# A block-causal attention and feed-forward kernel: the whole program in a scheduling block ordered by a simulated timeline, with the attention steps recorded scores first and attn*v in three steps

## The chip, the cores and the metric

The kernel runs on one core of a Trainium2 chip. The metric is the device time of one execution in microseconds (us); lower is better. Five engines work in the core, each through its own list of instructions in a fixed order, and they meet through semaphores: PE (TensorE, matmuls and transposes), DVE (VectorE), ACT (ScalarE), POOL (GpSimd) and SP (SyncE, which here issues all DMAs). An instruction that waits holds up everything behind it on its engine.

## The reference

```python
B, H, S, D = 8, 8, 576, 64                       # q, k, v; blocks of 64 for the mask
scores = q @ k.T / sqrt(D)                       # per batch and head
scores = where(block_i >= block_j, scores, -1e9)
attn = softmax(scores)                           # row maximum, exp, divided by its sum + 1e-9
x = concat_heads(attn @ v)                       # 4608 tokens x 512
h = x @ w_in                                     # 512 x 2048
g = where(h >= 1, h, where(h <= -1, 0, (h + 1)**2 / 4))
out = g @ w_out                                  # 2048 x 512
```

## The kernel before, in words

**Arithmetic.** Matmuls in full precision are slow on PE, so most operands are split into a high part of a shorter format (float32r) and the rest, and two or three matmuls take the place of one. The weights are split this way in the kernel (`convert`, L156, on ACT, DVE and POOL, in 64 pieces), mostly while the first batches are in work.

**Attention.** The unit is a *pair*: two heads (j = 0, 1) of one batch, so there are 8 x 4 = 32 pairs. Per head the 576 query rows make four tiles of 128 (in the groups 0: tiles 0 and 1, 1: tile 2, 2: tile 3), and the last 64 rows of both heads make one group more ("last"). So a pair has seven groups. Each goes through a chain:

- `scores` (L494) or `scores_last` (L518): matmuls into a PSUM bank `ps_s` (L482, L485; 24 of them in a pair); row maxima `nm` on DVE (L505, L529); exp on ACT (L509, L535) into `pr`, of which there are three buffers; sum and reciprocal `sm` on DVE (L491, L492); scaling on DVE (L515, L541). Then the result is copied by DMA into `prr` (L250, `as_float32r`), called the hop here.
- `turn` (L556) or `turn_last` (L572): PE transposes `prr` into a bank `ps_t` (L552); ACT and DVE split it into the tiles `pa` and `pb` (L545, L547). The last group's final 64 columns (the corner) go through a bank of their own into `pcs`.
- `attn_v_first` (L631) and `attn_v(0)`, `attn_v(1)` (L640): PE multiplies by v into `ps_av` (L591); ACT and DVE add two halves into `x32` (L613, L614), and `store_x` (L647) writes the split result to `xh`, `xl`, the input of the second part.

q and k of a pair are transposed too (`ps_qk`: L401, and L442 in `turned_last`, L437, for the last 64 rows). Pairs of the batches 0 and 1 are *plain* (no splits, other steps); those of the batches 2 to 7 are *far*, and their q and k are first copied from DRAM to DRAM (`fetch`, L273). From the middle of the second batch on, all these banks come from one ring of three (`work_bank`, L80). A bank is free again when the DVE or ACT instructions that read it are done.

**Feed-forward (FFN).** Nine chunks of 512 tokens, 16 pieces (fc) of 128 hidden columns each: `ffn_in` (L763) does 12 matmuls of 512 columns into the one bank `ph` (L770); ACT and DVE make `t` from it (L779, L780, L783), ACT and POOL split that into `gh`, `gl` (L784, L785); `ffn_out` (L790) does 12 matmuls into four banks `po` (L794, L799). So a piece has 24 matmuls. Chunk c takes tokens of batch c and for c over 0 also of batch c - 1; it can be done only when batch c is through the attention, all four pairs of it (the matmuls of one pair's channels, three of the first piece, can go before).

**Order.** `attention_steps` (L663) records each pair in eight steps, with the tail of the pair before and the head of the one after mixed in. From step 36 on (four pairs and four steps), one FFN step, that is half a piece, is recorded behind each attention step (L838 to L852): four pieces a pair, 16 a batch. The framework's scheduler then turns the recorded program into one list per engine; it may move instructions where dependencies and buffers allow. In the kernel before, this is done with its default method for the whole program.

Of the kernel before, what the change touches and what calls it, by code (L numbers as in the profile page):

```python
# [8 lines left out]
F32 = mybir.dt.float32  # L9
# [14 lines left out]
def block_attn_then_ffn(  # L24
# [61 lines left out]


    ident_f = ffn.tile([P, 512], F32, tag="t", name="ident_f")[:, :P]
    make_identity(nc, ident_f)
    ident_r = const.tile([P, P], F32R, tag="ident", name="ident_r")  # L90
    nc.vector.tensor_copy(ident_r, ident_f)
    ident = ident_r.bitcast(F32)

    xh = const.tile([P, NCC, RING], F32R, tag="xh", name="xh")
    xl = const.tile([P, NCC, RING], F32R, tag="xl", name="xl")
    wih = const.tile([P, NCC, DF], F32R, tag="wih", name="wih")
    wil = const.tile([P, NCC, DF], F32R, tag="wil", name="wil")

    copies = [dram.tile([B, H, S, D], F32, tag=f"raw{x}", name=f"raw{x}") for x in "qk"]
    wo_split = dram.tile([NFC, P, 2, DM], F32, tag="wo_split", name="wo_split")  # L100
# [3 lines left out]
    qa = const.tile([P, 2, QW], F32R, tag="qa", name="qa")  # L104
    qb = const.tile([P, 2, QW], F32R, tag="qb", name="qb")
    ka = const.tile([P, 2, S], F32R, tag="ka", name="ka")
    kb = const.tile([P, 2, S], F32R, tag="kb", name="kb")

    def last_blocks(t_):

        view = t_[:, :, SM : SM + BLK]
        if t_.shape[2] == S:
            return view
        part, (_, two), cols = view.ap
        return bass.AP(tensor=view.tensor, offset=view.offset, ap=[part, [QW + BLK, two], cols])


    mrow = att1.tile([NTL, 2, S], F32R, tag="pb0", name="mrow")


    pcs = [const.tile([P, 2, BLK], F32R, tag=f"pcs{i}", name=f"pcs{i}") for i in range(2)]
    vsr = [const.tile([P, NTL + 1, 2, D], F32R, tag=f"vsr{j}", name=f"vsr{j}") for j in range(2)]

    mtmp = ffn.tile([P, 512], F32, tag="t", name="mtmp")
    msel = ffn.tile([P, 512], F32, tag="t", name="msel")
    nc.vector.memset(mtmp, 0.0)
    nc.vector.memset(msel[:NTL], 0.0)
    nc.gpsimd.affine_select(
        out=msel[:NTL, : NTL * BLK].rearrange("p (t c) -> p t c", c=BLK),
        in_=msel[:NTL, : NTL * BLK].rearrange("p (t c) -> p t c", c=BLK),  # L130
        compare_op=ALU.not_equal, fill=1.0, base=0,
        pattern=[[-1, NTL], [0, BLK]], channel_multiplier=1,
    )
    sel = msel[:NTL, : NTL * BLK].rearrange("p (t c) -> p t c", c=BLK)
    for side in range(2):
        nc.vector.tensor_copy(mrow[:, side, :512], mtmp[:NTL, :512])
        nc.vector.tensor_copy(mrow[:, side, 512:S], mtmp[:NTL, : S - 512])
    rows = mrow[:, :, :SM].rearrange("p s (t c) -> p s t c", c=P)
    nc.vector.tensor_copy(rows[:, 0, :, :BLK], sel)
    nc.vector.tensor_scalar_mul(rows[:, 1, :, BLK:], sel, MASKED)  # L140
    for t_ in (qa, qb):
        nc.vector.tensor_copy(
            t_[:, :, SM:], mtmp[:, : 2 * (QW - SM)].rearrange("p (h c) -> p h c", h=2)
        )
    for t_ in pcs:
        nc.vector.tensor_copy(t_[BLK:], mtmp[BLK:, : 2 * BLK].rearrange("p (h c) -> p h c", h=2))
    for t_ in vsr:
        nc.vector.tensor_copy(
            t_[BLK:, NTL, :, :], mtmp[BLK:, : 2 * D].rearrange("p (h c) -> p h c", h=2)
        )  # L150
    for j in range(2):
        nc.sync.dma_start(qa[D:KA, j, :S].bitcast(F32), mrow[:, 0, :].bitcast(F32))
        nc.sync.dma_start(ka[D:KA, j, :].bitcast(F32), mrow[:, 1, :].bitcast(F32))


    def convert(n, source, hi, lo, done):  # L156

        if n < BORROW and n % 2:
            bits = ffn.tile([P, CW, 2], I32, tag="t", name="bits")
            work = ffn.tile([P, 2, CW], F32, tag="gl", name="work")  # L160
        else:
            bits = conv.tile([P, CW, 2], I32, tag="bits", name="bits")
            work = conv2.tile([P, 2, CW], F32, tag="work", name="work")
        nc.sync.dma_start(bits, source.bitcast(I32).rearrange("p (n t) -> p n t", t=2))
        top, mag = work[:, 0, :], work[:, 1, :].bitcast(U32)
        low = bits[:, :, 0]


        nc.scalar.mul(top, bits[:, :, 1].bitcast(F32), 2.0**-112)
        nc.scalar.mul(low, low.bitcast(U32), 2.0**-29)  # L170
        nc.vector.tensor_scalar(
            out=top, in0=top, scalar1=F32_TOP, scalar2=-F32_TOP, op0=ALU.min, op1=ALU.max
        )
        nc.vector.tensor_scalar(
            out=mag, in0=top.bitcast(U32), scalar1=3, scalar2=None, op0=ALU.logical_shift_left
        )
        nc.vector.scalar_tensor_tensor(
            out=mag, in0=top.bitcast(U32), scalar=0x80000000, in1=mag,
            op0=ALU.bitwise_and, op1=ALU.bitwise_or,
        )  # L180
        yield
        w32 = mag.bitcast(I32)
        nc.gpsimd.tensor_tensor(out=w32, in0=w32, in1=low, op=ALU.add)
        w32 = w32.bitcast(F32)
        nc.scalar.copy(hi(), w32)
        yield
        nc.gpsimd.tensor_tensor(out=lo(), in0=w32, in1=hi().bitcast(F32), op=ALU.subtract)
        if done:
            done()

    def weight_pieces():

        for f0 in range(0, DF, CW):
            fs = slice(f0, f0 + CW)
            for cc in range(NCC):
                yield (
                    w_in[cc * P : (cc + 1) * P, fs],
                    lambda cc=cc, fs=fs: wih[:, cc, fs], lambda cc=cc, fs=fs: wil[:, cc, fs], None,
                )
            for fc in range(f0 // P, (f0 + CW) // P):  # L200
                ws = {}

                def part(w, d0, ws=ws):
                    if not ws:
                        ws[0] = ffn.tile([P, 2, DM], F32R, tag="wo", name="ws")
                    return ws[0][:, w, d0 : d0 + CW]

                for d0 in range(0, DM, CW):
                    yield (
                        w_out[fc * P : (fc + 1) * P, d0 : d0 + CW],  # L210
                        lambda p_=part, d0=d0: p_(0, d0), lambda p_=part, d0=d0: p_(1, d0),
                        None if d0 + CW < DM else
                        lambda fc=fc, ws=ws: nc.sync.dma_start(wo_split[fc], ws[0].bitcast(F32)),
                    )

    def prepare_weights():

        live = []
        for n, piece in enumerate(weight_pieces()):
# [665 lines left out]
```

## Time and profile before

| what | value |
|---|---|
| median of 3 runs | 1267.56 us (1264.57 to 1269.79) |
| profiled execution, its own time | 1269.69 us |
| its span, first to last instruction | 1267.9 us |
| mean granted clock of PE | 0.981 |
| PE busy | 1200.1 us |
| DVE busy | 887.0 us |
| ACT busy | 703.2 us |
| POOL busy | 394.6 us |

The profile lists busy time per engine. A matmul's record overlaps the next one's, so the pace of PE is read from the starts of successive matmuls, not from their durations. The view by windows gives, for a stretch of time, the busy us of each engine with the number of instructions in brackets, the granted clock and the busy share of the DMA engines. The view of waits gives who waited for whom: total us, times, longest.

### The profile page before, as it was taken

The numbers are of one execution on the slowest core, as the hardware profiler recorded it, in microseconds if no ns is written. First come the engines' busy times: TensorE is split into PE (matmuls) and PEld (weight loads), VectorE is DVE, ScalarE is ACT, GpSimd is POOL, SyncE is SP. The second block draws the span as 40 slices with busy tenths as digits, with TensorE's granted clock in tenths as the row PEclk, the third lists the DMA queues.
The fourth block names the chain that finished last, engine by engine and source line by source line (L and its number), as shares of the span: only waits on it lengthen the run. The fifth ranks groups of instructions, "written<-read, shape, count | busy, mean of one in ns | idle before, by whom it ended". The sixth has DMA issues, their size and how long they took to land.

```text
span 1267.9 us, 20253 instructions
## 1 busy us (share of the span) xinstructions
PE 1200.1 (95%) x6280; PEld 998.8 (79%) x6280; DVE 887.0 (70%) x2188; ACT 703.2 (55%) x1827; POOL 394.6 (31%) x430
## 2 busy tenths in 40 slices
PE   5888889899999999999999999999999999999998
PEld 4666667678888888888888888888888888888886
DVE  8898877758777777777777777787777777322222
ACT  5787656646566655665656655566556555222222
POOL 3555655522222222222222222222222222222222
PEclk9888988999999999999999999999999999999999
DMA  5566666667888655555554655465556433422432
GB/s 158 167 176 215 203 228 197 217 198 237 260 273 266 215 162 158 154 175 163 156 162 145 187 157 152 138 189 153 160 154 190 137 128 118 132 87 98 133 100 100
DMA packets 185259, 215.43 MB, mean 170 GB/s; under 512 B 113840, under 2 KB 132272, under 8 KB 184384
## 3 DMA queue, kind: packets, MB, share of 16 engines
q1 hardware_dynamic: 185152, 214.14, 54.9%
q8 instruction: 50, 0.82, 0.3%
q14 instruction: 57, 0.47, 0.1%
HBM read 134.74 MB, written 31.98 MB: 131 GB/s over the span
## 4 chain that ended last, share of the span: by engine, by line
PE 69%; DVE 16%; ACT 6%; issue 5%; DMA 1%; POOL 1%; SPq 1%; ACTq 0%; POOLq 0%; DVEq 0%
PE ph L770 29%; PE po L794 15%; PE po L799 7%; PE ps_av L591 7%; PE ps_s L482 4%; ACT pr L509 3%; PE ps_s L485 3%; DVE t L780 2%; PE ps_t L552 2%; DVE t L783 2%; ACT t L779 2%; DVE pb L547 2%; DVE nm L505 2%; DVE sm L491 1%; DVE pr L515 1%
## 5 line engine op out<-in xcount | busy, mean ns | idle before, releaser
L785 POOL TENSOR_TENSOR gl<-t,gh 128x512 fp32r<-128x512 f32 x144 | 187.5, 1302 | 510.2 <-ACT gh L784 333.2
L794 PE MATMUL po<-wo,gh 128*128 128x512 f32 x1152 | 296.1, 397 | 0.5 <-DMA wo<-wo_split 0.3
L794 PEld LDWEIGHTS po<-wo,gh 128*128 128x128 f32 x1152 | 212.5, 189 | 44.5 <-DMA wo<-wo_split 0.7
L770 PE MATMUL ph<-xh,wih 128*128 128x512 f32 x576 | 232.9, 404 | 1.6 <-DVE t L783 1.6
L770 PE MATMUL ph<-xh,wil 128*128 128x512 f32 x576 | 228.8, 397 | 0.0
L770 PE MATMUL ph<-xl,wih 128*128 128x512 f32 x576 | 227.8, 396 | 0.5 <-DVE xl L627 0.5
L780 DVE SCALAR_TENSOR_TENSOR t<-t 128x512 f32<-128x512 f32 x144 | 101.5, 705 | 168.0 <-ACT t L779 165.2
L779 ACT ACTIVATE t<-ph 128x512 f32<-128x512 f32 x144 | 85.9, 597 | 173.8 <-PE ph L770 173.8
L509 ACT ACTIVATE pr<-ps_s,nm 128x128 f32<-128x128 f32 (+3 forms) x256 | 134.1, 527 | 60.5 <-DVE nm L505 58.4
L784 ACT CAST gh<-t 128x512 fp32r<-128x512 f32 x144 | 89.5, 621 | 120.3 <-DVE t L783 120.0
L799 PE MATMUL po<-wo,gl 128*128 128x512 f32 x576 | 155.6, 392 | 0.0
L482 PE MATMUL ps_s<-ka,qa 68*128 68x288 f32 (+4 forms) x384 | 135.3, 367 | 15.0 <-ACT pr L509 5.4
L379 POOL TENSOR_TENSOR vsr<-vn,vsr 128x256 fp32r<-128x256 f32 (+1 forms) x96 | 55.2, 576 | 246.2 <-ACT vsr L378 244.6
L770 PEld LDWEIGHTS ph<-xh,wil 128*128 128x128 f32 x576 | 109.5, 190 | 23.8
L770 PEld LDWEIGHTS ph<-xh,wih 128*128 128x128 f32 x576 | 109.8, 191 | 21.7 <-DVE t L783 2.3
L799 PEld LDWEIGHTS po<-wo,gl 128*128 128x128 f32 x576 | 108.7, 189 | 23.1
L505 DVE TENSOR_REDUCE nm<-ps_s 128x1 f32<-128x128 f32 (+3 forms) x256 | 118.8, 482 | 10.4 <-PE ps_s L485 9.4
L770 PEld LDWEIGHTS ph<-xl,wih 128*128 128x128 f32 x576 | 109.7, 190 | 20.5 <-DVE xl L627 0.9
L485 PE MATMUL ps_s<-kb,qb 128*128 128x288 f32 (+4 forms) x384 | 121.1, 322 | 0.0
L515 DVE TENSOR_SCALAR pr<-pr,sm 128x128 f32<-128x128 f32 (+3 forms) x256 | 107.3, 440 | 5.4
L783 DVE TENSOR_TENSOR t<-ph,t 128x512 f32<-128x512 f32 x144 | 98.7, 686 | 2.2
L491 DVE TENSOR_SCALAR sm<-sm 128x1 f32<-128x1 f32 (+1 forms) x224 | 52.0, 232 | 68.3 <-ACT pr L509 65.7
(111 smaller groups left out, 1871.4 us busy)
## 6 DMA issues: line engine op xcount, KB each, us to landing
wo<-wo_split SPq DMA_DIRECT2D x144, 512.0 KB, 3.5
prr<-pr SPq DMA_DIRECT2D x96, 192.0 KB, 2.5
prr<-pr SPq DMA_DIRECT2D x72, 256.0 KB, 2.8
out_dram<-ob SPq DMA_DIRECT2D x36, 256.0 KB, 2.9
bits<-in_moe_w_in_dram SPq DMA_DIRECT2D x32, 256.0 KB, 3.5
bits<-in_moe_w_out_dram SPq DMA_DIRECT2D x32, 256.0 KB, 3.0
wo_split<-ws SPq DMA_DIRECT2D x16, 512.0 KB, 2.9
qa<-qb SPq DMA_DIRECT2D x63, 128.0 KB, 2.4
```

Of the source, the lines that this page charges most:

```text
L482: nc.tensor.matmul(ps, qa[:KA, j, c0 : c0 + P], ka[:KA, j, k0 : k0 + n], start=first, stop=False)
L485: nc.tensor.matmul(ps, qb[:, j, c0 : c0 + P], kb[:, j, k0 : k0 + n], start=False, stop=last)
L505: nc.vector.tensor_reduce(out=nm[:, i : i + 1], in_=ps[:, cs], axis=AX.X, op=ALU.max, negate=True)
L509: nc.scalar.activation(pr[:, cs], ps[:, cs], AF.Exp, bias=nm[:, i : i + 1], scale=1.0, accum_out=sm[:, i : i + 1],)
L515: nc.vector.tensor_scalar_mul(pr[:, cs], pr[:, cs], sm[:, i : i + 1])
L770: nc.tensor.matmul(ph, w[:, cc, fs], x[:, cc, xs], start=(cc == 0 and i == 0), stop=(cc == NCC - 1 and i == 2),)
L779: nc.scalar.activation(t_, ph, AF.Relu, bias=0.5, scale=0.5)
L780: nc.vector.scalar_tensor_tensor(out=t_, in0=t_, scalar=1.0, in1=t_, op0=ALU.min, op1=ALU.mult)
L783: nc.vector.tensor_tensor(out=t_, in0=ph, in1=t_, op=ALU.max)
L785: nc.gpsimd.tensor_tensor(out=gl, in0=t_, in1=gh.bitcast(F32), op=ALU.subtract)
L794: nc.tensor.matmul(po[tt], gh[:, ts_], wo[:, w, :], start=(fc == 0 and w == 0), stop=False)
L799: nc.tensor.matmul(po[tt], gl[:, ts_], wo[:, 0, :], start=False, stop=fc == NFC - 1)
```

## The change

Three things, in one edit:

1. The body of the kernel, from the identity matrix to the last FFN step, stands in `with tc.block(schedule_with_timeline_sim=True):`, so that a simulated timeline of the engines sets the order of each list.
2. For the far pairs the steps are recorded in another order: the scores of a step come ahead of its transposes; the hop is recorded at the step's end (`move`); the three parts of attn*v stand in the first three steps of the following pair (`attn_v(0)`, `attn_v_first`, `attn_v(1)`); `turned_last` of the next pair moves to the sixth step of the pair before it.
3. The corner is transposed into the free quarter of the bank of `turn(1, 0)` instead of a bank of its own; `xtmp` is one tile for both halves in `attn_v_first`.

```diff
+    with tc.block(schedule_with_timeline_sim=True):
...
-            self.pr[j, g] = as_float32r(pr[:, : cols[-1].stop], self.plain) if self.hop else [pr]
+                self.pr[j, g] = [pr[:, : cols[-1].stop]]
+                if not self.far:
+                    self.moved(j, g)
+
+            def moved(self, *key):
+                if self.hop:
+                    self.pr[key] = as_float32r(self.pr[key][0], self.plain)
+
+            def move(self, *key):
+                if self.far:
+                    self.moved(*key)
...
             for c0 in range(0, n, P):
                 self.transposed(ps[:, c0 : c0 + P], pr, c0, P)
+                if self.far and j == 1 and g == 0:
+                    self.turn_corner(self.pr.pop(("last",)), ps[:BLK, n : n + P])
...
-            if far:
-                old.turn(1, 1)
             if cur:
                 cur.scores(0, 0)
...
             if far:
-                old.attn_v_first()
+                    old.turn(1, 1)
+                    old.attn_v(0)
+                if cur:
+                    cur.move(0, 0)
             yield
-            if far:
-                old.turn(1, 2)
             if cur:
                 cur.scores(0, 1)
+                    if not cur.raw:
                 cur.turned_last()
...
+                if far:
+                    old.turn(1, 2)
+                    old.attn_v_first()
+                if cur:
+                    cur.move(0, 1)
             yield
             if far:
+                    if cur:
+                        cur.scores(0, 2)
                 old.attn_v(1)
                 old.store_x()
...
             if cur.far:
                 cur.begin()
-                cur.turn(0, 0)
                 cur.scores_last()
+                    cur.turn(0, 0)
...
-            if cur.far:
-                cur.turn(0, 1)
-                cur.scores(1, 0)
-            else:
-                cur.scores(1, 0)
-                cur.turn(0, 2)
+                cur.scores(1, 0)
+                cur.turn(0, 1 if cur.far else 2)
+                cur.move(1, 0)
...
             if nxt:
                 nxt.turned(False, 0)
+                    if nxt.raw:
+                        nxt.turned_last()
...
             if cur.far:
                 cur.turn(1, 0)
-                cur.attn_v(0)
```

The edit moves lines, so an instruction has another line number in the changed program (L770 is L798 there, L794 is L822, L799 is L827, L482 is L483, L552 is L566, L591 is L609, L442 is L443). Each engine's list holds the same number of instructions as before (6170 on PE, matmul by matmul); only their places differ. All lists change nearly everywhere. Three places follow.

PE, in the seven groups of the pair that ends batch 2 (pair 11 of 0 to 31), after its scores of the last group; `ph` and `po` are FFN, all else attention. Before:

```order
L552 MATMUL ps_t<-ident_r,prr 128x128 x3
L482 MATMUL ps_s<-ka,qa 128x128
L485 MATMUL ps_s<-kb,qb 128x128
L482 MATMUL ps_s<-ka,qa 128x256
L485 MATMUL ps_s<-kb,qb 128x256
L401 MATMUL ps_qk<-ident_r,qk 128x128 x4
L794 MATMUL po<-wo,gh 128x512 x8
L799 MATMUL po<-wo,gl 128x512 x4
L552 MATMUL ps_t<-ident_r,prr 128x128 x4
L482 MATMUL ps_s<-ka,qa 128x384
L485 MATMUL ps_s<-kb,qb 128x384
L770 MATMUL ph<-xh,wih 128x512
```

And the changed program, at the same pair:

```order
L566 MATMUL ps_t<-ident_r,prr 128x128 x3
L402 MATMUL ps_qk<-ident_r,qk 128x128 x4
L483 MATMUL ps_s<-ka,qa 128x384
L486 MATMUL ps_s<-kb,qb 128x384
L566 MATMUL ps_t<-ident_r,prr 128x128 x4
L443 MATMUL ps_qk<-ident_r,qk 128x128
L483 MATMUL ps_s<-ka,qa 128x512
L486 MATMUL ps_s<-kb,qb 128x512
L566 MATMUL ps_t<-ident_r,prr 128x128 x7
L566 MATMUL ps_t<-ident_r,prr 64x128
L402 MATMUL ps_qk<-ident_r,qk 128x128 x4
L483 MATMUL ps_s<-ka,qa 128x128
```

Before, 12 FFN matmuls stand after every three or four attention items; at this place of the changed program there are none, and L443 stands among the groups of the pair before its own. Counted from one pair's last group to the next one's, before has 96 FFN matmuls in every far pair. The changed program has, for the pairs that follow pair 8, 111, 144, 126 and 3, then 108, 144, 129 and 3, and so on to the end: the 16 pieces of a batch stand in about three pairs, and the fourth has none. It has five stretches of PE's list in which no four FFN matmuls stand together, with 40, 42, 32, 38 and 42 score matmuls in them, 194 in all (24 make a pair), and 6, 11, 6, 11 and 6 FFN matmuls.

PE, the end of the attention in pair 31. Before:

```order
L794 MATMUL po<-wo,gh 128x512 x8
L799 MATMUL po<-wo,gl 128x512 x4
L552 MATMUL ps_t<-ident_r,prr 128x128 x3
L591 MATMUL ps_av<-pb_12815,vsr_111 128x320
L591 MATMUL ps_av<-pb_12816,vsr_111 128x320
```

Changed:

```order
L483 MATMUL ps_s<-ka,qa 128x512
L486 MATMUL ps_s<-kb,qb 128x512
L566 MATMUL ps_t<-ident_r,prr 128x128 x7
L566 MATMUL ps_t<-ident_r,prr 64x128
L566 MATMUL ps_t<-ident_r,prr 128x128 x3
L609 MATMUL ps_av<-pb_12770,vsr_112 128x320
```

Before, FFN of chunk 6 stands between the last groups; in the changed program it is used up, and from the last group of pair 31 to its last attn*v only three FFN matmuls follow.

SP, the DMA queue, where the first of the 48 DRAM copies of q and k (`rawq`, `rawk`) stands. Before:

```order
L787 DMA wo<-wo_split 128x1024
L339 DMA kn<-in_k_dram 64x64 x2
L164 DMA bits<-in_moe_w_out_dram 128x512
L243 DMA vsr_111<-pr 128x512
L164 DMA bits<-in_moe_w_out_dram 128x512 x2
L282 DMA rawq<-in_q_dram 16x4608
```

Changed:

```order
L165 DMA bits<-in_moe_w_out_dram 128x512 x2
L335 DMA qn<-in_q_dram 128x2x256
L340 DMA qn<-in_q_dram 64x64 x2
L283 DMA rawq<-in_q_dram 16x4608
L165 DMA bits<-in_moe_w_out_dram 128x512
L335 DMA kn<-in_k_dram 128x2x256
```

Before, the copies stand in rows 134 to 394 of SP's list, behind FFN loads (`wo`) and hops (`pr`); in the changed program they stand in rows 23 to 144, the first ones among the loads of pairs 1 and 2.

1293 lines of the change are left out of this document (650 added, 643 removed).

## The prediction

> **What bounds the kernel now.** I began with the page's busy times and then asked for busy time by windows, cut where the busy pattern of the page changes. The page:
>
> ```profile
> PE 1200.1 (95%) x6280; PEld 998.8 (79%) x6280; DVE 887.0 (70%) x2188; ACT 703.2 (55%) x1827; POOL 394.6 (31%) x430
> ```
>
> The windows (length; then busy us of PE, PE's weight loads, DVE, ACT and POOL, granted clock, DMA share, GB/s):
>
> ```profile
> 32.00:128.00 96.00, 80.76 (x434) 64.51 (x433) 85.80 (x258) 75.08 (x227) 50.91 (x63) 0.89 0.62 186
> 0.00:256.00 256.00, 209.07 (x1019) 164.98 (x1020) 210.85 (x578) 170.62 (x496) 135.70 (x171) 0.92 0.63 194
> 256.00:1056.00 800.00, 784.18 (x4329) 662.96 (x4329) 611.40 (x1500) 477.38 (x1229) 210.75 (x222) 1.00 0.59 178
> 311.70:1047.00 735.30, 721.65 (x4004) 611.74 (x4004) 568.69 (x1396) 442.42 (x1140) 196.32 (x206) 1.00 0.58 176
> 1120.00:1152.00 32.00, 32.00 (x143) 26.44 (x142) 8.30 (x12) 7.32 (x12) 7.69 (x6) 1.00 0.28 91
> ```
>
> There are three stages. Up to 256 us there is attention with little FFN, and PE idles 46.9 us; DVE is the fuller engine (85.80 of 96 us, 0.894, in the densest part, 0.824 over the whole stage). From 256 to 1056 us attention and FFN run mixed, and PE idles only 15.8 of 800 us: PE sets the pace, DVE has 24% to spare. After that comes FFN alone with PE full (143 matmuls in 32 us). So the middle stage is at PE's own pace because FFN matmuls lie beside each pair's work on DVE. That cover is what the change touches.
>
> What one far pair costs each engine: the window 311.70:1047.00 runs from one `L442` to another, and the groups of DVE in it give 22 pairs and the softmax rows.
>
> ```profile
> L505 DVE TENSOR_REDUCE nm<-ps_s 128x1 f32<-128x384 f32 (+3 forms) x176 | 81.1, 482 | 0.7
> L515 DVE TENSOR_SCALAR pr<-pr,sm 128x128 f32<-128x128 f32 (+3 forms) x176 | 64.4, 387 | 4.4
> L491 DVE TENSOR_SCALAR sm<-sm 128x1 f32<-128x1 f32 (+1 forms) x154 | 39.0, 253 | 59.9 <-ACT pr L509 57.8
> L492 DVE RECIPROCAL sm<-sm 128x1 f32<-128x1 f32 (+1 forms) x154 | 25.3, 164 | 5.1
> L541 DVE TENSOR_SCALAR pr<-pr,sm 128x576 f32<-128x576 f32 x22 | 11.5, 521 | 0.8
> ```
>
> The same window for the instructions on FFN's `t`, and on the output tiles `ob` (columns: DVE, ACT, POOL; then DVE, ACT):
>
> ```profile
> 311.70:1047.00 735.30, 121.00 (x176) 107.12 (x176) 114.57 (x88) 1.00 0.58 176
> ```
>
> ```profile
> 311.70:1047.00 735.30, 6.85 (x10) 5.87 (x10) 1.00 0.58 176
> ```
>
> DVE's attention work is (568.69 - 121.00 - 6.85) / 22 = 20.04 us a pair. ACT's is (442.42 - 107.12 - 5.87) / 22 = 15.0 us, so DVE is the one that limits attention left alone. The four softmax rows L505 to L492 are 209.8 us; over 22 pairs with six groups each that is 1.59 us a group.
>
> For PE the timeline gives the pace (start, us, instruction):
>
> ```profile
> 603.66 0.53 PE L401 MATMUL ps_qk<-ident_r,qk 128*128 128x128 f32 x4
> 604.03 0.46 PE L770 MATMUL ph<-xh,wih 128*128 128x512 f32 x1
> 604.33 0.39 PE L770 MATMUL ph<-xl,wih 128*128 128x512 f32 x1
> ...
> 612.55 0.25 PE L442 MATMUL ps_qk<-ident_r,qk 128*128 128x128 f32 x1 [0.38 <-DVE x L614]
> ...
> 621.37 0.39 PE L770 MATMUL ph<-xh,wih 128*128 128x512 f32 x1
> ...
> 623.91 0.39 PE L770 MATMUL ph<-xh,wil 128*128 128x512 f32 x1
> ```
>
> The first and the twelfth matmul of a half piece start 2.54 us apart, so one takes 0.231 us. A pair lasts 735.30 / 22 = 33.4 us, its 96 FFN matmuls 22.2, PE's idle time (735.30 - 721.65) / 22 = 0.6, so attention takes 10.6 us of PE. That is half of DVE's 20.04. A pair without FFN beside it leaves PE idle for about 10 us, and PE's time is not to be had back, since the last 32 pieces run with PE full anyway.
>
> **The change part by part.**
>
> *FFN runs ahead in PE's list.* The order shows it: the 16 pieces of a batch now stand in three pairs, and then the list has attention alone until the next batch is through, because a chunk can't begin before. Five such stretches hold 194 score matmuls, 194 / 24 = 8.08 pairs, and 40 FFN matmuls. PE's work in them is 8.08 x 10.6 + 40 x 0.231 = 94.8 us. DVE's is 8.08 x 20.04 = 161.9 us. PE's list can't get past a transpose before DVE, ACT and the hop have delivered its group, so DVE's work can't lag far: three buffers `pr` let at most three groups' softmax spill over a stretch's end, 5 x 3 x 1.59 = 24 us. The stretches are worth, in time beyond PE's own work: with DVE never idle, 161.9 - 24 - 94.8 = 43 us; with DVE as full as in the first stage's densest part, 161.9 / 0.894 - 24 - 94.8 = 62 us; at the whole first stage's 0.824, 161.9 / 0.824 - 24 - 94.8 = 78 us. I take 62, as that part is also a pipeline of pairs with almost no FFN. The denser pairs lose nothing: six pieces put 33.3 us of FFN beside them on PE, and DVE has 20.04 + 6 x 1.375 = 28.3 us in 43.9.
>
> *The end of attention.* The last pair's second half had 12-matmul runs between its groups and now has three FFN matmuls. There DVE's half pair (10 us), then one group's chain (0.482 + 0.253 + 0.164 + 0.387 and 2.5 for the hop, in the page's row below, 3.8 us without the exp) and about 3 us of attn*v, which nothing overlaps, stand against some 7 us of PE work. I take +10, between 4 (chain hidden) and 13.
>
> ```profile
> prr<-pr SPq DMA_DIRECT2D x96, 192.0 KB, 2.5
> ...
> rawq<-in_q_dram SPq DMA_DIRECT2D x24, 288.0 KB, 5.1
> rawk<-in_k_dram SPq DMA_DIRECT2D x24, 288.0 KB, 4.8
> ```
>
> *Scores first, and L443's new place.* PE's waits from 260 to 1080 us:
>
> ```profile
> PE ps_qk L442 <- DVE x L614: 8.9, 23, 0.4
> PE ps_s L482 <- ACT pr L509: 5.2, 17, 0.3
> ```
>
> They are waits for a bank, 8.9 of them once a pair for one that `x32`'s additions read. L443's bank is now the one `turned_raw` used, three uses earlier and long read. I let all 15.8 us of the middle stage's idle time go where FFN still covers a pair, two thirds of the pairs: -10.5 (bounds 0 and -15.8). A matmul right behind transposes starts 0.07 us late (604.03 to 604.33 against 0.231). PE's list has 264 places where another kind of work follows a transpose, 319 before: 55 x 0.07 x 2/3 = -2.5. The corner's bank saved frees one of 22 uses of the ring a pair; it is worth nothing where PE doesn't wait, and belongs to the stretches otherwise. The order of hops behind scores costs nothing under cover of FFN; in the stretches it is in DVE's 0.894.
>
> *The first stage.* Its PE list differs little. The 48 DRAM copies now queue among the first pairs' loads on SP, each some 5 us on its way where a hop takes 2.5, while the DMA share there is 0.63: between 0 and +15, taken at +3, since DVE and not a load ends most waits there. DVE's new order could also win part of PE's 46.9 us idle, at most about half, since DVE itself has 211 us to do in 256; from that, -23 to 0, taken at 0.
>
> *PE's clock.* In the first stage PE idles and the clock falls:
>
> ```profile
> 40.00:48.00 8.00, 5.22 (x33) 3.86 (x31) 7.94 (x23) 6.71 (x21) 4.49 (x7) 1.00 0.67 184
> 48.00:56.00 8.00, 5.64 (x23) 4.96 (x24) 7.28 (x24) 5.52 (x17) 5.40 (x7) 0.61 0.52 139
> ```
>
> but over 96 us it is 0.89, so PE's 94.8 us would grow by 12, still under DVE's 157. I add nothing. [...] The first stage, with its mean of 0.89, shows drops but no lasting half rate.
>
> *Sum:* 62 + 10 - 13 + 3 = +62 us. It is a difference, worked out within the profiled execution (1269.69 us, 1.8 us around its span, 2.1 above the median); on the median of 1267.56 it gives **1330 us**.
>
> **The rivals.**
>
> - *Banks, not DVE, bound the stretches.* A far pair takes 21 uses of three banks. If each is held 4 us, because every read of a bank queues behind other work on a full DVE, a pair takes 28 us: 8.08 x 28 - 24 - 94.8 = 107, in all +107, 1375 us. For it: no `po` bank helps there, as in most of the first stage. Against: a group's reads (L505 twice, the exp, under 2 us) are short. Chance 0.16.
> - *The clock halves in the stretches.* PE's 94.8 become 190 us, the bound there, and its loss is 95: +95, 1362 us. [...] Chance 0.07.
> - *The first stage gains what it can.* The new order wins 23 us there, all else as forecast: 1304 us. Chance 0.10.
> - *Faster: the deeper pipeline fills the stretches.* Scores now stand three groups ahead of their transposes instead of two. If DVE's surplus could wait for the next FFN run, a stretch would take PE's time alone and the gains stay: 4 - 18, some 1253 us. This decides from a mean stretch under about 22 us (19 is PE's part) instead of 31. It needs 13 us of DVE work carried over a stretch's end, eight groups, where `pr` has three buffers. Chance 0.07.
> - *No change.* The smallest stretches (43), the smallest end (4) and the largest gains (-18 and -23): +6 us, 1274. That the change does not do what it says is excluded: the lists differ as shown. Chance 0.04.
>
> **How the numbers follow.** The forecast (stretches at DVE's pace, 1284 to 1350) has 0.56. About 0.5% (6 us) is what a measurement of this kernel can tell from no change. Faster is 0.07, the same 0.04, slower the rest, 0.89. The low end is 43 + 4 - 18 - 12 (half of what the first stage could gain) = +17, 1284 us; it leaves out the two cases at the other side, 0.11. The high end takes in the banks' 1375 and 10 us more for the upper price of the copies, 1385 us.
>
> **What would show it right or wrong.** In the changed kernel's profile the windows must show five dips of PE in the middle stage, 25 to 40 us long, one about every fourth pair, with PE near 0.6 busy and DVE near 0.9; between them PE full and L443 without its wait; a sixth short dip before FFN alone. Dips with DVE at 0.7 and PE waiting for PSUM banks would be the banks' rival; a granted clock near 0.5 through the dips, the clock's. PE at 0.95 or more through the middle stage would make the prediction wrong in its main step, and so would a first stage ended 20 us sooner or later.

## The result, and the profile after

The changed program took 1413.62 us (median of 4 runs, 1408.54 to 1416.58), the program before 1267.84 us beside it: a ratio of 1.1146, interval 1.1127 to 1.1164, or 146 us more. Forecast were 1330 us, 62 us more, and at most 1385. So the direction was right and the size too small by 84 us. The profiled execution has a span of 1410.6 us, 142.7 above before's.

The page of the changed program: busy time, and PE's busy share, the granted clock and the DMA share in 40 slices of 35.3 us.

```profile
PE 1266.7 (90%) x6280; PEld 1050.2 (74%) x6280; DVE 902.9 (64%) x2188; ACT 711.9 (50%) x1827; POOL 393.1 (28%) x430
...
PE   5776898899997899969998999889997999799998
...
PEclk9778999899998799969997899889995999799999
DMA  6896576655444445444454444445454443222423
```

The forecast dips are there: behind the first stage PE's row falls in the 13th, 18th, 22nd, 26th and 31st slice, and in the 35th just before FFN stands alone. The granted clock falls at the same places. Unexpected is the 9 in the third slice of the DMA row.

The five dips by windows, with the piece between the first two of them ahead (length; busy us of PE, its weight loads, DVE, ACT, POOL; granted clock, DMA share, GB/s):

```profile
482.00:588.00 106.00, 105.81 (x558) 89.22 (x558) 71.88 (x165) 54.39 (x135) 26.60 (x26) 1.00 0.49 148
436.00:482.00 46.00, 34.44 (x165) 27.93 (x165) 34.79 (x89) 25.92 (x74) 8.21 (x12) 0.70 0.43 127
594.00:642.00 48.00, 33.76 (x155) 26.92 (x156) 36.40 (x94) 26.10 (x72) 7.67 (x9) 0.72 0.41 125
748.00:798.00 50.00, 40.48 (x184) 33.12 (x184) 39.36 (x103) 29.03 (x79) 7.45 (x8) 0.73 0.48 141
900.00:946.00 46.00, 35.34 (x172) 29.67 (x171) 37.00 (x98) 28.33 (x79) 8.94 (x12) 0.74 0.43 130
1052.00:1102.00 50.00, 39.50 (x175) 32.07 (x174) 39.42 (x105) 29.49 (x82) 8.12 (x10) 0.69 0.44 134
```

Between dips PE is full (105.81 of 106 us). In a dip neither engine is: PE is busy for 0.70 to 0.81 of the time, DVE for 0.76 to 0.80 (34.79 / 46 the least, 37.00 / 46 the most). Forecast were PE near 0.6 and DVE near 0.9. No engine is full, so something between them must be looked for. PE's waits in the first dip (in the changed program L510 and L547 are the exp, L396 makes a low part of k, L631 adds the halves of `x32`, L561 makes a low part of `pa` or `pb`; each reads a bank):

```profile
PE ps_t L566 <- issue: 2.9, 2, 1.6
PE ps_s L483 <- ACT pr L547: 2.4, 2, 1.2
PE ps_s L483 <- ACT pr L510: 2.0, 3, 1.1
PE ps_qk L443 <- DVE kb L396: 1.4, 1, 1.4
...
PE ps_s L483 <- DVE x L631: 1.1, 2, 0.8
```

Each line has the instruction that PE can't start and what released it; "issue" is a wait for nothing that the profile shows. Scores (L483) and the transposes of q and k (L443) wait for a reader to leave a bank: 2.4 + 2.0 + 1.4 + 1.1 = 6.9 us of the 46.00 - 34.44 = 11.6 that PE idles. Such waits are not all: in the second dip the longest is one of 3.2 us for a hop. PE waiting for banks is what the prediction gave as the sign of the banks' rival, with DVE at 0.7, a little lower than it is here.

**Where the 142.7 us are.** Two landmarks cut both spans into three stages: the last start of `xl` in a plain pair, and in a far pair. They are the last time in each row (shortest, median, longest ns; first to last start). Before:

```profile
L627 DVE TENSOR_TENSOR xl<-ps_av,xh x16: 409/453/493, 33.9 to 280.7; 128x256 fp32r<-128x256 f32 x8, 128x320 fp32r<-128x320 f32 x8
L657 POOL TENSOR_TENSOR xl<-x,xh x32: 591/1212/1427, 319.5 to 1085.1; 128x576 fp32r<-128x576 f32 x16, 128x384 fp32r<-128x384 f32 x8, 128x192 fp32r<-128x192 f32 x8
```

And the changed program:

```profile
L644 DVE TENSOR_TENSOR xl<-ps_av,xh x16: 408/448/492, 43.0 to 318.5; 128x256 fp32r<-128x256 f32 x8, 128x320 fp32r<-128x320 f32 x8
L675 POOL TENSOR_TENSOR xl<-x,xh x32: 591/1208/1434, 360.6 to 1226.0; 128x576 fp32r<-128x576 f32 x16, 128x384 fp32r<-128x384 f32 x8, 128x192 fp32r<-128x192 f32 x8
```

The first stage lasts 318.5 instead of 280.7 us (+37.8), the middle 907.5 instead of 804.4 (+103.1), the rest 184.6 instead of 182.8 (+1.8). But the first stage also holds more FFN now. These are PE's instructions on `ph` in it, then those on `po`, before:

```profile
0.00:280.70 280.70, 55.83 (x183) 0.92 0.64 196
0.00:280.70 280.70, 45.56 (x168) 0.92 0.64 196
```

and changed:

```profile
0.00:318.50 318.50, 57.66 (x201) 0.89 0.69 221
0.00:318.50 318.50, 52.39 (x192) 0.89 0.69 221
```

That is 393 FFN matmuls instead of 351, and 42 x 0.231 = 9.7 us that the middle no longer has to do. Net of them the first stage lost 28.1 us and the middle 112.8.

### The profile page after: what moved, and what is told of

Its sections match the earlier page's. It is cut to its first block, busy times and chain, and to the rows that moved or that the text cites. A ratio compares the mean times of both kernels' runs of the same rounds, so it can differ in the third digit from the quotient of the medians.

```text
span 1410.6 us, 20280 instructions
## 1 busy us (share of the span) xinstructions
PE 1266.7 (90%) x6280; PEld 1050.2 (74%) x6280; DVE 902.9 (64%) x2188; ACT 711.9 (50%) x1827; POOL 393.1 (28%) x430
## 4 chain that ended last, share of the span: by engine, by line
PE 72%; DVE 11%; DMA 7%; issue 4%; ACT 3%; POOL 2%; SPq 1%; ACTq 0%; POOLq 0%; DVEq 0%
PE ph L798 27%; PE po L822 18%; PE po L827 9%; PE ps_av L609 8%; PE ps_s L483 4%; PE ps_t L566 3%; PE ps_s L486 3%; DVE pr L516 1%; DVE nm L506 1%; DMA rawk<-in_k_dram 1%; DVE work L178 1%; PE ps_qk L402 1%; DMA wo<-wo_split 1%; DVE pb L561 1%; DMA kn<-in_k_dram 1%
## 5 line engine op out<-in xcount | busy, mean ns | idle before, releaser
L822 PE MATMUL po<-wo,gh 128*128 128x512 f32 x1152 | 302.1, 397 | 3.9 <-DMA wo<-wo_split 2.9
L822 PEld LDWEIGHTS po<-wo,gh 128*128 128x128 f32 x1152 | 213.6, 189 | 47.0 <-DMA wo<-wo_split 3.2
L798 PE MATMUL ph<-xh,wih 128*128 128x512 f32 x576 | 236.6, 411 | 10.0 <-DVE t L811 6.4
L798 PE MATMUL ph<-xl,wih 128*128 128x512 f32 x576 | 233.1, 405 | 1.0 <-POOL xl L675 1.0
L798 PE MATMUL ph<-xh,wil 128*128 128x512 f32 x576 | 232.6, 404 | 0.0
L483 PE MATMUL ps_s<-ka,qa 68*128 68x288 f32 (+4 forms) x384 | 145.6, 391 | 41.4 <-DMA ka<-kb 12.8
L827 PE MATMUL po<-wo,gl 128*128 128x512 f32 x576 | 162.1, 397 | 0.0
L510 ACT ACTIVATE pr<-ps_s,nm 128x128 f32<-128x128 f32 (+3 forms) x256 | 134.1, 527 | 55.0 <-DVE nm L506 54.0
L798 PEld LDWEIGHTS ph<-xh,wih 128*128 128x128 f32 x576 | 111.9, 194 | 35.4 <-DVE t L811 8.3
L486 PE MATMUL ps_s<-kb,qb 128*128 128x288 f32 (+4 forms) x384 | 130.8, 347 | 0.0
L798 PEld LDWEIGHTS ph<-xh,wil 128*128 128x128 f32 x576 | 112.1, 195 | 23.4
L798 PEld LDWEIGHTS ph<-xl,wih 128*128 128x128 f32 x576 | 112.6, 196 | 22.3 <-POOL xl L675 1.3
L483 PEld LDWEIGHTS ps_s<-ka,qa 68*128 68x128 f32 x384 | 81.6, 212 | 58.3 <-issue 16.7
L827 PEld LDWEIGHTS po<-wo,gl 128*128 128x128 f32 x576 | 107.4, 190 | 21.4
L566 PEld LDWEIGHTS ps_t<-ident_r,prr 128*128 128x128 f32 x600 | 73.1, 150 | 51.0 <-issue 20.3
L380 POOL TENSOR_TENSOR vsr<-vn,vsr 64x64 fp32r<-64x64 f32 (+1 forms) x96 | 51.2, 540 | 213.1 <-ACT vsr L379 212.9
```

The costliest lines, as they stand in the source:

```text
L483: nc.tensor.matmul(ps, qa[:KA, j, c0 : c0 + P], ka[:KA, j, k0 : k0 + n], start=first, stop=False)
L486: nc.tensor.matmul(ps, qb[:, j, c0 : c0 + P], kb[:, j, k0 : k0 + n], start=False, stop=last)
L510: nc.scalar.activation(pr[:, cs], ps[:, cs], AF.Exp, bias=nm[:, i : i + 1], scale=1.0, accum_out=sm[:, i : i + 1],)
L566: nc.tensor.transpose(out.bitcast(F32R), src, ident_r)
L798: nc.tensor.matmul(ph, w[:, cc, fs], x[:, cc, xs], start=(cc == 0 and i == 0), stop=(cc == NCC - 1 and i == 2),)
L822: nc.tensor.matmul(po[tt], gh[:, ts_], wo[:, w, :], start=(fc == 0 and w == 0), stop=False)
```

## The experiments

The theory: the block lets FFN run ahead, the list then has stretches without cover, and attention alone is slower there than forecast. The size has several possible causes: the low clock, the banks, DVE, and something in the first stage. The stages of each kernel are cut at the same two landmarks:

| kernel | time, us | ratio to before (interval) | first stage | middle | rest |
|---|---|---|---|---|---|
| before | 1267.84 | | 280.7 | 804.4 | 182.8 |
| changed | 1413.62 | 1.1146 (1.1127 to 1.1164) | 318.5 | 907.5 | 184.6 |
| e1, block alone | 1446.28 | 1.1412 (1.1390 to 1.1434) | 317.1 | 940.5 | 184.3 |
| e2, steps alone | 1273.17 | 1.0049 (1.0031 to 1.0067) | 278.6 | 808.8 | 182.7 |
| e3, FFN held | 1282.84 | 1.0120 (1.0104 to 1.0135) | 302.8 | 794.9 | 184.4 |
| e4, copies held | 1391.24 | 1.0971 (1.0940 to 1.1001) | 296.9 | 905.0 | 184.9 |
| e5, both held | 1269.08 | 1.0003 (0.9990 to 1.0016) | 291.7 | 794.2 | 184.3 |
| e6, less DVE work | 1388.74 | 1.0951 (1.0920 to 1.0983) | 314.7 | 884.7 | 184.1 |
| e11, conversions too | 1265.94 | 0.9983 (0.9969 to 0.9997) | 284.9 | 794.6 | 184.4 |

### Block and steps apart (e1, e2)

e1 puts the body of the kernel before, otherwise untouched, in the block:

```diff
+    with tc.block(schedule_with_timeline_sim=True):
...
```

> The steps of the kernel before, recorded unchanged, in the block ordered by the simulated timeline. In PE's list the FFN runs ahead again: per far pair 120, 160, 100 and 3 FFN matmuls, five stretches without cover. Theory (the block's order makes the loss, by stretches without FFN and by the DRAM copies drawn into the first stage): 1380 to 1440 us, with five dips of PE as in the changed kernel. Rival (the steps recorded in another order make it): within 15 us of 1268. Split evenly between the two: about 1340.

e2 is the changed program without the block:

```diff
-    with tc.block(schedule_with_timeline_sim=True):
+    if True:
```

> The changed kernel's steps without the block: the default order. PE's list has 96 FFN matmuls in each far pair, as before. Theory: within 10 us of 1268, a little under it if the waits for banks go (up to -13). Rival (the steps make the loss): 1380 us or more.

The block alone costs 178 us, more than the whole change and 6 us above the range expected. Its list runs FFN ahead like the changed one: counted as in the change's section, its far pairs have about 120, 160, 100 and 3 FFN matmuls, where e2 has 96 in each. The steps alone cost 5 us and gain nothing. Inside the block they win 33 us of the middle (940.5 to 907.5). By PE's timeline 23 of the 33 lie where FFN is missing: the five stretches last 208.8 us in e1 and 198.5 in the changed program, and the uncovered end of attention 31.9 against 19.2. Both the groups' places and the FFN's differ there, so no run says which of the two it is.

### FFN held to its pair (e3)

Each FFN step is put behind the PE instruction recorded last, so the simulated timeline can't draw it forward; all else stays in its hands.

```diff
-                next(ffn_steps, None)
+                pe = [x for x in nc.cur_bb.bb.instructions if x.engine == mybir.EngineType.PE]
+                with tc.issue_after(pe[-1]):
+                    next(ffn_steps, None)
```

> The changed kernel with each FFN step's PE instructions queued behind the last PE instruction of the attention step recorded ahead of it, an order on PE's list alone: 96 FFN matmuls in each far pair again, the first stage without FFN, the copies still early. Theory: the middle stage comes back to about 33.5 us a pair, some 100 us are won, and the loss of the first stage (some 30 us) stays: 1290 to 1315 us. If the run-ahead were not the cause: about 1410 us.

This gives back 131 of the 146 us, 7 us more than the range expected allows. The window over the middle of e3, and then over that of the changed program:

```profile
303.00:1097.00 794.00, 784.73 (x4377) 674.33 (x4376) 624.51 (x1509) 475.35 (x1230) 209.27 (x220) 1.00 0.53 159
```

```profile
319.00:1226.00 907.00, 840.98 (x4349) 708.35 (x4347) 626.77 (x1508) 484.92 (x1230) 205.11 (x219) 0.92 0.46 140
```

With nearly the same number of instructions (4377 on PE, 4349), PE idles 9.3 us in e3 and 66.0 in the changed program; and it is busy 56 us longer in the latter, at a granted clock of 0.92 instead of 1.00. DVE's work is the same in both. The middle of e3 is 9.5 us shorter than before's: so much the steps and the block's order win together where FFN covers the pairs (e2's, with the steps alone, is 4.4 us longer).

### The copies held (e4), and both (e5)

The 48 DRAM copies are put behind the DMA recorded last before each, which moves them from the rows 23 to 144 of SP's list to 183 to 851.

```diff
-                        nc.sync.dma_start(dst, src)
+                        sp = [x for x in nc.cur_bb.bb.instructions if x.engine == mybir.EngineType.SP]
+                        with tc.issue_after(sp[-1]):
+                            nc.sync.dma_start(dst, src)
```

> The changed kernel with each of the 48 DRAM copies of q and k queued on SP behind the DMA recorded ahead of it, so that the copies stand in rows 183 to 851 of SP's list instead of 23 to 144; the stretches without FFN stay. Theory (the early copies fill the DMA engines in the first stage and delay its loads): 20 to 35 us won there, 1375 to 1395 us. Rival (the first stage loses by the new order of DVE and POOL, not by DMA): within 8 us of 1413.

> Both orders held in the changed kernel: FFN steps queued on PE behind their attention step, and the 48 DRAM copies queued on SP behind the DMA recorded ahead of them. Theory: the gains add up, about 20 us less than with the FFN order alone (1282.8): 1258 to 1270 us, so at or a little under the kernel before. If the first stage loses by the block's order of DVE and POOL rather than by the copies: 1275 to 1285 us.

The copies cost 21.6 us (318.5 to 296.9) in the changed program and 11.1 with FFN held (302.8 to 291.7), about half of what was expected there. The window from 64 to 128 us of the changed program, then of e4:

```profile
64.00:128.00 64.00, 43.11 (x200) 33.49 (x199) 48.47 (x138) 39.57 (x119) 28.58 (x37) 0.81 0.93 322
```

```profile
64.00:128.00 64.00, 52.22 (x267) 42.36 (x267) 53.46 (x165) 43.80 (x133) 28.85 (x38) 0.83 0.56 163
```

With the copies early the DMA engines are busy for 0.93 of this time and PE gets 200 matmuls done instead of 267. The chain of waits of the changed program says who stands in it (start, us, what):

```profile
92.15 8.31 DMA rawk<-in_k_dram
...
101.67 5.09 DMA rawk<-in_k_dram
...
115.03 6.66 DMA kn<-in_k_dram
...
127.13 5.90 DMA ka<-kb
```

The loads that the first pairs need (`kn`) and a transfer inside the core (`ka`) last longer than 5 us in this chain, beside copies that no one wants before the far pairs; a large `kn` load took 6.1 us in the median, and 2.8 in the kernel before. And PE's longest wait in the first 260 us is for such a transfer (total, times, longest):

```profile
PE ps_s L483 <- DMA ka<-kb: 12.8, 2, 8.6
```

### DVE's part (e6)

Two of DVE's instructions are left out of each step that splits q and k of the far pairs (the low parts of q and k are not computed, so the scores are less exact).

```diff
-                nc.vector.scalar_tensor_tensor(
-                    out=lo, in0=ps[:D], scalar=SCALE, in1=hi.bitcast(F32),
-                    op0=ALU.mult, op1=ALU.subtract,
-                )
...
-                nc.vector.tensor_tensor(out=lo, in0=ps[D:], in1=hi.bitcast(F32), op=ALU.subtract)
```

> The changed kernel without the two DVE instructions per transposed bank that make the low parts of q and k in far pairs (left out of the computation; the matmuls read what stands there). 3.3 us of DVE less in a pair, none of it on the softmax chain. Theory of the prediction (the stretches without FFN are at DVE's pace): 8.08 pairs x 3.3 = 27 us less, 1380 to 1392 us. Rival (the stretches are at the pace of PE at half clock and of the chain): under 10 us less, 1403 to 1413 us.

It took 1388.74 us, a ratio of 1.0951 (1.0920 to 1.0983), 25 us less than the changed program. That is inside the range expected if DVE sets the pace, and yet it does not show that. The block ordered the lists anew: counted as in the change's section, e6's five stretches hold 170 score matmuls (7.08 pairs) and 29 FFN matmuls instead of 194 and 40. By PE's timeline they last 164.1 us instead of 198.5. Without their FFN matmuls (0.231 us each) that is 22.2 us a pair instead of 23.4: a pair became 1.2 us shorter, where 3.3 us of DVE's work were left out. And the same two instructions read the bank `ps_qk` (L396 is one of them, for which PE waits 1.4 us in the first dip), so without them the bank comes free sooner, and the banks' theory has a gain as well.

### Attention alone: clock against banks (e7 to e10, e12)

Here the disputed price is measured by itself. In e7 the FFN is left out (the output gets other data); e8 adds five matmuls of 512 columns on constants behind each attention step, which only keep PE busy. e9 and e12 are e8 and e7 with all of attention's banks from the ring and the four `po` banks in turn, seven in place of three. e10 is e9 with six buffers for `pr` and for what goes with it (to make room, the low part of the first weights shares the tile of the high part).

```diff
-        ffn_steps = feed_forward()
...
-                next(ffn_steps, None)
-        for _ in ffn_steps:
-            pass
+        for r0 in range(0, NT, P):
+            nc.sync.dma_start(out[r0 : r0 + P, :], wih[:, 0, :512].bitcast(F32))
```

```diff
+                pe = [x for x in nc.cur_bb.bb.instructions if x.engine == mybir.EngineType.PE]
+                with tc.issue_after(pe[-1]):
+                    ph = ps_h.tile([P, 512], F32, tag="ph", name="ph")
+                    for n in range(5):
+                        nc.tensor.matmul(ph, ident_r, wih[:, n % NCC, :512], start=True, stop=True)
```

```diff
-                banks["free"] = False
+                pass
```

```diff
-    att3 = ctx.enter_context(tc.tile_pool(name="att3", bufs=3))
+    att3 = ctx.enter_context(tc.tile_pool(name="att3", bufs=6))
...
-    conv = ctx.enter_context(tc.tile_pool(name="conv", bufs=3))
-    conv2 = ctx.enter_context(tc.tile_pool(name="conv2", bufs=3))
+    conv = ctx.enter_context(tc.tile_pool(name="conv", bufs=6))
+    conv2 = ctx.enter_context(tc.tile_pool(name="conv2", bufs=6))
...
-        wil = const.tile([P, NCC, DF], F32R, tag="wil", name="wil")
+        wil = wih
```

> The changed kernel without the whole FFN (left out: both matmul layers; the output is filled with other data): 24 far pairs of attention in a row. It measures what a pair takes when nothing covers it. The prediction's price was 22.4 us a pair at DVE 0.89 busy; the stretches of the changed kernel look like 28 to 29. Theory now (PE's clock is down in the stretches): 26 to 30 us a pair, granted clock 0.5 to 0.7, DVE 0.65 to 0.75 busy.

> The same without FFN, but with five matmuls of 512 columns on constant data behind each attention step, queued on PE behind that step (9.2 us of PE a pair, 19.8 with attention's 10.6). They need nothing and nobody needs them. Clock theory: the granted clock rises to 0.9 or more and a pair takes 22 to 25 us, less than without them though PE has more to do. Rival (banks and the chain's latency): the clock rises and a pair takes as long as without them or longer.

> Attention alone with the constant matmuls (no FFN, left out), and the work banks taken in turn from the ring of three and from the four that FFN no longer needs, so seven in place of three. With three it took 25.6 us a pair at full clock and DVE 0.84 busy. If banks hold it back: 22 to 23.5 us a pair. If it is the chain through DVE and ACT: 25 to 26 us.

> As the last one, and six buffers in place of three for the softmax result, for its copy and for the two pools that the copy lands in (the low part of the first layer's weights shares the high part's place, since nothing reads it). If three buffers limit how far the scores run ahead of their transposes: 1 us a pair or more below seven banks alone. Else the same within 0.5 us.

> Attention alone, without FFN (left out) and without the constant matmuls, on seven work banks: the fourth case of three or seven banks, with or without matmuls that keep PE's clock up. 26.9 us a pair with three banks and no such matmuls, 25.6 with three and them, 20.2 with seven and them. If the banks are the main limit: 20 to 23 us a pair, whatever the clock is. If the clock counts as much once banks are free: 24 to 27 us at a clock near 0.6.

One run each; they took 934.20, 910.45, 773.02, 774.75 and 799.07 us. What counts is the period of a far pair. L443's weight load occurs once in each of 24 far pairs, so the first and last start in its row give 23 periods. e7:

```profile
L443 PEld LDWEIGHTS ps_qk<-ident_r,qk x24: 183/183/184, 271.2 to 889.9; 128*128 128x128 f32 x24
```

(889.9 - 271.2) / 23 = 26.90 us. In the same way e8, e9, e10 and e12:

```profile
L443 PEld LDWEIGHTS ps_qk<-ident_r,qk x24: 138/139/142, 279.2 to 867.1; 128*128 128x128 f32 x24
```

```profile
L443 PEld LDWEIGHTS ps_qk<-ident_r,qk x24: 138/141/146, 270.2 to 734.3; 128*128 128x128 f32 x24
```

```profile
L443 PEld LDWEIGHTS ps_qk<-ident_r,qk x24: 138/140/145, 269.9 to 736.0; 128*128 128x128 f32 x24
```

```profile
L443 PEld LDWEIGHTS ps_qk<-ident_r,qk x24: 138/143/227, 258.8 to 753.8; 128*128 128x128 f32 x24
```

The clock in them, from a window inside the far pairs, e7, e8, e9 and e12 in turn:

```profile
302.00:842.00 540.00, 371.28 (x1732) 321.75 (x1730) 421.53 (x1108) 306.52 (x872) 71.20 (x108) 0.58 0.40 113
```

```profile
302.00:842.00 540.00, 443.94 (x2654) 369.93 (x2655) 454.27 (x1161) 316.96 (x916) 78.21 (x113) 0.99 0.42 118
```

```profile
302.00:702.00 400.00, 395.62 (x2502) 342.81 (x2501) 373.48 (x1090) 296.86 (x859) 72.10 (x108) 1.00 0.53 151
```

```profile
302.00:702.00 400.00, 297.89 (x1572) 264.79 (x1571) 360.33 (x1006) 272.70 (x791) 65.52 (x97) 0.65 0.49 139
```

Together, us for a far pair with nothing beside it:

| | three banks | seven banks |
|---|---|---|
| no fill | 26.90 (clock 0.58) | 21.52 (clock 0.65) |
| PE kept busy | 25.56 (clock 0.99) | 20.18 (clock 1.00) |

Four more banks are worth 5.4 us a pair at either clock; filling PE, and with it the clock, is worth 1.3 with either number of banks. The 1.3 is what is left after the filling's own time on PE, so the clock by itself may be worth more. And the 5.4 is the banks' worth together with the order that the block makes when it has them: e7 and e8 have attention's 2824 matmuls in the same order on PE, but e12 has the same kind of matmul as e7 at only 1318 of the 2824 places. DVE is busy for 0.78 of the time in e7 (421.53 / 540), as in the dips, for 0.90 in e12 (360.33 / 400) and for 0.93 in e9. Of the ranges expected, e7's, e10's and e12's times came true; e8's 25.56 lies between its two theories, and e9's 20.18 is below both. The waits of PE in e8, where the clock is full, name the banks:

```profile
PE ps_qk L443 <- DVE pb L561: 29.4, 21, 1.4
PE ps_s L483 <- ACT pr L547: 20.1, 21, 1.2
PE ps_av L609 <- DVE kb L396: 18.4, 21, 0.9
PE ps_qk L402 <- DVE pb L561: 17.7, 19, 0.9
```

About once a pair each of four kinds of matmul waits for a read of the bank it is to have next: 85.6 us of the 96.1 that PE idles in this window, so in e8 itself, with e7's order, banks are what PE waits for. The two largest waits of e9 in the same view are small and name no bank:

```profile
PE ps_t L566 <- DMA prr<-pr: 1.9, 4, 0.7
PE ps_t L566 <- DVE sm L492: 1.1, 2, 0.6
```

e10's 20.27 us say that the `pr` buffers are no limit with seven banks; but PE is full in e9 (395.62 of 400 us), so they might have been hidden there, and with three banks it wasn't tried.

### The order of the conversions (e11)

e5 still has a first stage 11 us longer than before's. Here the weight conversions of each step stay behind that step's last instruction on DVE.

```diff
-            for _ in range(want - converted):
-                next(weights, None)
+            dve = [x for x in nc.cur_bb.bb.instructions if x.engine == mybir.EngineType.DVE]
+            with tc.issue_after(dve[-1]):
+                for _ in range(want - converted):
+                    next(weights, None)
```

> The kernel with both orders held (1269.1 us), and each step's weight conversions queued on DVE behind that attention step's DVE work. Its middle stage is 10 us shorter than before's and its first stage 11 longer. If DVE's order of conversions makes that: first stage 5 to 11 us shorter, 1258 to 1264 us, a version faster than both kernels. If not: within 4 us of 1269.

It wins 6.8 us of the first stage (291.7 to 284.9), as expected, but the time of 1265.94 us is 2 us above the range. It is 0.17% under before's, the interval just clear of 1: a difference too small to call this version faster.

## Why the prediction was right and wrong

By the steps of its sum, on the profiled spans, with e3 as the changed program without FFN run ahead. What the missing cover costs is the two middles' difference and the FFN done early: 907.5 - 794.9 + 9.7 = 122.3 us. PE's timeline splits it. The first stretch, from its first matmul to the run of FFN behind it, and then that run:

```profile
436.87 1.03 PE L609 MATMUL ps_av<-pa,vsr 128*128 128x256 f32 x8
...
475.78 0.79 PE L798 MATMUL ph<-xh,wih 128*128 128x512 f32 x1
476.37 0.63 PE L798 MATMUL ph<-xl,wih 128*128 128x512 f32 x1
476.80 0.63 PE L798 MATMUL ph<-xh,wil 128*128 128x512 f32 x1
...
479.63 0.40 PE L798 MATMUL ph<-xh,wih 128*128 128x512 f32 x1
479.86 0.40 PE L798 MATMUL ph<-xl,wih 128*128 128x512 f32 x1
```

It lasts 38.9 us; the others last 45.6, 34.9, 36.7 and 42.4, together 198.5, or 103.7 beyond the 94.8 of PE's own work in the prediction. The FFN behind it starts at 0.43 us a matmul (476.37 to 476.80) and comes to its 0.23 only 4 us later: the clock stays low for a while after the stretch (0.50 from 476 to 479 us). Against 0.231 a matmul the first twelve behind the five stretches lose 8.3 us. The end of attention:

```profile
1206.86 0.38 PE L566 MATMUL ps_t<-ident_r,prr 128*128 128x128 f32 x3
...
1215.98 0.70 PE L566 MATMUL ps_t<-ident_r,prr 128*128 128x128 f32 x4 [3.23 <-DMA prr<-pr]
...
1226.02 0.49 PE L798 MATMUL ph<-xh,wih 128*128 128x512 f32 x1 [1.74 <-ACT xh L674]
```

These are 19.2 us, 12.2 beyond the prediction's estimate of 7 us of PE work; the longest wait is one for a hop. Stretches and end leave 6.4 of the 122.3 us, and the slow FFN's 8.3 more than account for them.

| step | forecast | measured |
|---|---|---|
| stretches | +62 | +103.7 |
| end of attention | +10 | +12.2 |
| what is left of the 122.3 | 0 | +6.4 |
| pairs under cover of FFN | -13 | -9.5 |
| first stage | +3 | +28.1 |
| FFN alone | 0 | +1.8 |
| sum | +62 | +142.7 |

**Right: the mechanism.** FFN runs ahead in PE's list, five dips and a sixth follow, and their length is lost time. e1 shows that the block does it, e3 that without the run-ahead the loss of the middle is gone. Also right: between dips PE is full, and L443 doesn't wait there; the end of attention cost about what was forecast, and the covered pairs win most of it (9.5 us in e3, where all pairs are covered, against 13 forecast for two thirds of them).

**Wrong: the price of a pair in a stretch.** The step that failed is "with DVE as full as in the first stage's densest part", 20.04 / 0.894 = 22.4 us a pair. Attention alone takes 26.90. In the forecast's own sum that is 8.08 x 26.9 - 24 - 94.8 = 98.6 us instead of 62, and the timeline has 103.7: a stretch lasts 39.7 us in the mean, where the prediction had 31. The first stage was the wrong model. Its pairs are plain, and until step 36, so through most of its densest part, attention has the `po` banks as well, while in a stretch the ring has three. (Step 36 lies in the middle of the second batch's first pair, not of the batch; its scores start at 110 us in the kernel before.) The prediction named this difference under its banks' rival and still took the price from there. With seven banks 21.52 us were measured and DVE 0.90 busy, close to the 22.4 and 0.894 that it had supposed. The banks' rival had the mechanism and, at 28 us a pair, nearly the price; it was held to be unlikely because one group's reads are short. What e8's waits show is that reads of several kinds hold the banks up in turn: not the last group's exp alone (L547, 20.1 us), but the splits of the transposed `prr` and of k too (L561 with 47.1, L396 with 18.4).

**Wrong: the first stage.** The step "taken at +3", between 0 and +15, measured +28.1: the copies 21.6 (e4), above their upper bound, and 6.5 by the other orders. In e5, which is 11.0 us above before's first stage, e11 finds the conversions' place to be worth 6.8. The forecast priced a copy as one transfer beside a hop, with the DMA share at 0.63; but 48 of them drawn close together took it to 0.93. The stage ended 37.8 us later, which the prediction had named among the signs of being wrong.

**The clock.** It fell, to 0.69 to 0.74 in the dips, as the rival said, but it was not the bound. By e7 and e8 it is 8.08 x 1.3, or some 11 us, of the stretches' 103.7, net of what the filling takes; "I add nothing" also left out the 8.3 us behind them. No run shows its whole worth, but with seven banks a pair took 21.52 us at a clock of 0.65, less than three banks allow at 0.99. PE's longest wait in e7 is in this row:

```profile
PE ps_s L483 <- ACT pr L547: 41.3, 20, 2.4
```

e7's granted clock was 0.58 in the mean, and in that window PE never waited longer than 2.4 us; no run shows what sets the clock. The 95 us that the clock's rival worked out, with the clock halved through the stretches and PE as the bound, did not come: in the first dip the clock is at 0.50 from 446 to 462 us, but the means of the five are 0.69 to 0.74, and PE is busy for 0.69 of e7's window (371.28 / 540).

**The range.** Banks (1375) and first stage (25 us above the forecast's +3) came together, near 1400 us; the range took each rival by itself.

**Open.** The price of e7 explains 98.6 of the stretches' 103.7 us, with the 24 us of DVE work carried over their ends as the prediction supposed; no run measures the 24. How much of the price is the clock's is known only net of the filling, 1.3 us a pair.

## What to carry to other kernels

A scheduler that fills every idle moment of an engine with ready work spends the cover of later, barer stretches; count the filler between two dependencies in the new list, and tie it to its place if it piles up. Price such a stretch by the resources that it has itself, the banks above all (here four more were worth 5.4 us a pair, 26.90 to 21.52), and not by another stage that looks alike; two cheap runs with one of them enlarged settle which counts. A prefetch that depends on nothing can be drawn to the front as well, where it takes DMA time from the loads that are wanted now (here 21.6 us, with a DMA share of 0.93 instead of 0.56 from 64 to 128 us).

## What the runs showed of the hardware

A granted clock of 0.58 instead of 0.99 cost 1.3 us of 27 where PE waits for banks anyway (26.90 against 25.56 us a pair, the latter with the filling on PE besides). PE's busy time was larger at the lower clock, 841.0 us at 0.92 in the middle stage of the changed program against 784.7 at 1.00 in e3's, so a busier PE was no sign there that PE is the bound. In e7's far pairs the clock was 0.58, with no wait of PE above 2.4 us. The clock stayed low for some 2 to 5 us of FFN work behind a stretch of the changed program (0.50 from 476 to 479 us, matmuls 0.43 us apart). In the kernel before, at a clock of 1.00, four matmuls of 320 columns in full precision took 2.11 us in a plain pair's attn*v (L591, eight records from 58.79 to 60.90 us), or 0.53 each; eight in float32r took 1.15 us in a far pair's (602.35 to 603.50), or 0.144 each. And in the changed program the DMA share from 96 to 112 us reads above one:

```profile
96.00:112.00 16.00, 11.76 (x47) 9.00 (x46) 10.35 (x31) 6.94 (x22) 7.70 (x9) 0.79 1.03 383
```

At 383 GB/s, PE did 47 matmuls in 16 us there.
